# The opening of a top-k attention and gated FFN kernel: loads in the program's order, weight splits behind score evictions, the first unit one step sooner

## The chip, the cores and the metric

One core of one Trainium2 chip. The metric is the device time of one execution in microseconds. The engines are PE (TensorE), DVE (VectorE), ACT (ScalarE), POOL (GpSimd) and SP (SyncE, which here issues nearly all loads).

## What is computed

The reference, cut: attention over 8 batches and 8 heads of 576 positions with 64 columns each. Every row of scores keeps those that are at least its 32nd largest. The result, as a 4608 x 512 matrix, goes through a gated FFN of width 1536.

```python
scores = scale * np.matmul(q, k.transpose(0, 1, 3, 2))
kth = np.partition(scores, -top_k, axis=-1)[..., -top_k:-top_k + 1]
attn = softmax(np.where(scores >= kth, scores, -1e9))
x = np.matmul(attn, v)            # then laid out as (4608, 512)
out = (1 / (1 + np.exp(-(x @ w_gate))) * (x @ w_val)) @ w_out
```

## The kernel before

**Steps.** `run` (L532) goes through 160 steps; a step is a pair of heads `p` (4 of them), and a tile `i` of 128 query rows (tile 4 has 64 rows of each head and counts as one). Names end in `_i_p` (`e_1_3` is tile 1 of the pair 3). In the first batch steps 0 to 7 are tiles 0 and 1 of the four pairs, 8 to 15 tiles 2 and 3, 16 to 19 tile 4. The 256 rows of steps 0 to 7 are the first unit of the FFN.

**One step** passes through four stages on all engines:

- *scores* (L256): PE multiplies (`pss`), ACT evicts to `s` (L270 in the first batch, in two halves).
- *select* (L334): DVE takes the 8 largest of eight segments (`cand`, L351, 16 instructions), and from them the 24 largest of the row (`tops`, `leads`, L355, L357). ACT marks what lies under the 24th (`under`, L364), POOL multiplies (`u`, L370, L371). Then DVE takes the threshold (`kths`, L378). ACT makes the exponentials (`e`, L300), DVE masks and sums them (`masked`, L305 to L309), POOL spreads the inverse sum (`inv`, L311).
- *turn* (L381): PE transposes `e` and `inv` (`pt`, L389, L392), ACT evicts (`et`, L395).
- *weigh* (L415): PE multiplies with the values (`po`, L425), DVE scales (`xf`, L429), ACT and POOL cut that into a high and a low part (`xh` L432, `xl` L433), which are the FFN's input.

At step `n` the loop (L642) puts out the scores of step `n + 2`, the select of `n`, the mask of `n - 1`, the turn of `n - 2` and the weighing of `n - 3`.

**FFN.** `ffn` (L436) is a generator, which `more` (L578) carries on to a goal: a number of rows that follows the attention's progress by the table `PACE` (L78). Its projections are `pz` (L466 to L468: 3 matmuls per slab of 128 inputs, 12 per weight), their gates come from ACT (L473), DVE (L476), ACT (L477) and POOL (L478).

**Weights.** The weights arrive as 64-bit numbers, which must be cut into two parts of 32 bits on the chip: 18 weights in two halves. A half is a *split*: a load (`wraw`, L149), then `split_front` (L151: ACT L168, L173, L176; DVE L169 to L171; POOL L175), then `split_back` (L179: PE `wrest` L183 to L185, ACT L187, a store to `ws`). The splits of the first `LOADED` = 5 weights stand in steps 0 to 9, one half at each, and these weights are loaded again for the first unit (`w_first`, L195, `first_weights` L198). The other weights are split while the first unit's FFN runs and used straight from the split.

**What sets the order.** PE's order is the program's (`manual_schedule`, L628). On the other engines a scheduler places each instruction by its own estimate of times; `urgent` (L124) gives a priority, and `first_scores` (L121) holds an instruction behind the eviction of some scores of the first steps. Loads on SP are placed in the same way. Each engine and SP's queue then runs its list strictly in order: an instruction that waits holds up what is behind it.

## Time and profile before

| | us |
|---|---|
| median of 3 runs | 1597.29 |
| lowest and highest run | 1595.20 and 1598.22 |
| the profiled execution, its own time | 1597.74 |
| its span in the trace | 1595.9 |
| busy in the span: PE, PE weight loads, DVE, ACT, POOL | 1522.6, 1427.3, 1285.6, 1165.3, 1124.2 |

The page's slices (40 us each) show PE at 3, 7, 7 and 8 tenths in the first four and at 9 or more in nearly all others. PE is thus the engine of most of the span, and 73 of its 1595.9 us are idle. DVE is at 6 in the first slice and at 9 or more in the next three.

### The profile page before, as it was taken

Reading aid. Unit: us, or ns where it says so; the run is one execution under the profiler, and the core shown is the slowest. Engines: PE = TensorE matmul, PEld = TensorE weight load, DVE = VectorE, ACT = ScalarE, POOL = GpSimd, SP = SyncE. Lnnn points to the kernel's source line nnn. Section 1 sums busy time; section 2 is a strip of 40 time slices with the busy share of each in tenths; the row PEclk is TensorE's granted clock in tenths of the full one; section 3 lists DMA queues with packets and bytes.
Section 4 is the critical chain, followed back from the end, with each engine's and each line's share of the span. In section 5 each row is a group of like instructions: output and inputs, shape, how many; then the busy total and the mean of one; then the engine's idle time right before and its main releaser. Section 6 shows DMA issues by size and latency. Waiting matters only on the chain.

```text
span 1595.9 us, 36725 instructions
## 1 busy us (share of the span) xinstructions
PE 1522.6 (95%) x11810; PEld 1427.3 (89%) x11810; DVE 1285.6 (81%) x5940; ACT 1165.3 (73%) x2567; POOL 1124.2 (70%) x1747
## 2 busy tenths in 40 slices
PE   3779899999999999999999999999999999999998
PEld 1457679989999999999999999999999999999998
DVE  6999877898998788899899788899899788898001
ACT  5878887788787677787777677787777777777321
POOL 3667896698886786797776886797776786685312
PEclk9989999999999999999999999999999999999999
DMA  7456778777755565666555665666555665554575
GB/s 215 154 197 229 263 263 285 269 246 255 254 194 187 212 240 198 213 211 222 190 200 189 211 242 197 213 213 219 189 200 191 211 226 198 198 192 168 188 267 187
DMA packets 91739, 342.94 MB, mean 215 GB/s; under 512 B 10256, under 2 KB 37392, under 8 KB 63248
## 3 DMA queue, kind: packets, MB, share of 16 engines
q1 hardware_dynamic: 86352, 321.62, 58.2%
q10 hardware_dynamic: 5184, 18.88, 3.0%
q8 instruction: 95, 1.56, 0.4%
q14 instruction: 108, 0.88, 0.2%
HBM read 312.15 MB, written 28.31 MB: 213 GB/s over the span
## 4 chain that ended last, share of the span: by engine, by line
PE 69%; DVE 10%; ACT 3%; POOL 2%; issue 2%; DMA 1%; SPq 0%; ACTq 0%; POOLq 0%; DVEq 0%
PE pz L466 10%; PE pz L468 10%; PE pz L467 10%; PE pss L284 8%; PE po L425 7%; PE pt L389 6%; PE po L490 5%; PE po L492 5%; PE po L491 5%; DVE cand L351 3%; DVE e L305 2%; DVE kths L378 2%; DVE cand L357 1%; PE pt L400 1%; ACT under L364 1%
## 5 line engine op out<-in xcount | busy, mean ns | idle before, releaser
L370 POOL TENSOR_TENSOR u<-s,under 128x288 f32<-128x288 f32 x576 | 420.1, 753 | 98.9 <-ACT under L364 94.4
L466 PE MATMUL pz<-xh,w 128*128 128x384 f32 (+1 forms) x1152 | 404.4, 351 | 1.3 <-DMA w<-ws 1.3
L351 DVE MAX8 cand<-s 128x8 f32<-128x72 f32 x2304 | 348.0, 217 | 70.0 <-ACT s L292 55.8
L468 PE MATMUL pz<-xh,w 128*128 128x384 f32 (+1 forms) x1152 | 377.2, 327 | 0.0
L467 PE MATMUL pz<-xl,w 128*128 128x384 f32 (+1 forms) x1152 | 376.3, 327 | 0.0
L305 DVE SCALAR_TENSOR_TENSOR e<-s,kths,e 128x576 f32<-128x576 f32 x288 | 285.9, 995 | 22.1 <-ACT e L300 21.7
L364 ACT ACTIVATE under<-s,leads 128x576 fp8e4<-128x576 f32 x288 | 222.5, 774 | 95.2 <-DVE leads L355 83.8
L378 DVE MAX8 kths<-u 128x8 f32<-128x584 f32 x288 | 218.9, 760 | 58.9 <-POOL u L371 56.7
L300 ACT ACTIVATE e<-s,st 128x576 f32<-128x576 f32 x288 | 210.5, 771 | 34.3 <-PE pt L389 18.8
L466 PEld LDWEIGHTS pz<-xh,w 128*128 128x128 f32 x1152 | 217.1, 188 | 5.1 <-issue 2.1
L467 PEld LDWEIGHTS pz<-xl,w 128*128 128x128 f32 x1152 | 217.8, 189 | 0.0
L478 POOL TENSOR_TENSOR gl<-gf,gh 128x384 fp32r<-128x384 f32 (+1 forms) x156 | 153.4, 983 | 90.1 <-ACT gh L477 86.8
L468 PEld LDWEIGHTS pz<-xh,w 128*128 128x128 f32 x1152 | 216.6, 188 | 0.0
L395 ACT ACTIVATE et<-pt 128x384 f32<-128x384 f32 (+1 forms) x384 | 197.3, 524 | 20.1 <-PE pt L389 14.8
L490 PE MATMUL po<-gh,w 128*128 128x384 f32 (+1 forms) x576 | 203.9, 354 | 0.8 <-ACT part L505 0.7
L389 PE MATMUL pt<-ident,e 128*128 128x128 f32 x1152 | 191.6, 276 | 9.1 <-ACT et L395 9.0
L491 PE MATMUL po<-gl,w 128*128 128x384 f32 (+1 forms) x576 | 188.6, 328 | 3.1 <-POOL gl L478 3.1
L492 PE MATMUL po<-gh,w 128*128 128x384 f32 (+1 forms) x576 | 189.0, 328 | 0.0
L425 PEld LDWEIGHTS po<-et,v 128*64 128x64 f32 x1600 | 160.4, 137 | 16.5 <-issue 11.6
L425 PE MATMUL po<-et,v 128*64 128x128 f32 (+1 forms) x1600 | 173.5, 265 | 0.0
L426 PE MATMUL po<-et,v 128*64 128x128 f32 (+1 forms) x1600 | 173.5, 265 | 0.0
L389 PEld LDWEIGHTS pt<-ident,e 128*128 128x128 f32 x1152 | 146.0, 141 | 30.4 <-ACT et L395 12.7
(104 smaller groups left out, 3471.0 us busy)
## 6 DMA issues: line engine op xcount, KB each, us to landing
w<-ws SPq DMA_DIRECT2D x216, 1024.0 KB, 4.9
v<-in_v_dram SPq DMA_DIRECT2D x68, 320.0 KB, 3.5
wraw<-in_w_dram SPq DMA_DIRECT2D x36, 512.0 KB, 4.5
ws<-wsplit ACTq DMA_DIRECT2D x36, 512.0 KB, 3.9
qraw<-in_q_dram SPq DMA_DIRECT2D x140, 128.0 KB, 3.5
kraw<-in_k_dram SPq DMA_DIRECT2D x56, 288.0 KB, 3.8
out_dram<-acc SPq DMA_DIRECT2D x40, 192.0 KB, 4.3
w_first<-ws SPq DMA_DIRECT2D x5, 1024.0 KB, 4.8
```

The costliest lines, as they stand in the source:

```text
L305: nc.vector.scalar_tensor_tensor(e[:, j], s[:, j], kth[j], e[:, j], op0=ALU.is_ge, op1=ALU.mult, accum_out=st[:, 4 + j : 5 + j])
L351: nc.vector.max(cand[:, j, 8 * g : 8 * g + 8], s[:, j, g * SEG : (g + 1) * SEG])
L370: nc.gpsimd.tensor_tensor(u[:, j, c], s[:, j, c], under[:, j, c], op=ALU.mult)
L378: nc.vector.max(kths[:, at[j] : at[j] + 8], u[:, j])
L389: nc.tensor.transpose(pt[:, c], ef[:, k0 : k0 + P], ident)
L425: nc.tensor.matmul(po[D:, c], vt[:, 5 + a], et[:, 4 + a, :n], start=a == 0, stop=a == 4)
L466: nc.tensor.matmul(ps[:, R], wt[:, u, 0, d], xh[:, R], start=d == 0, stop=False)
L467: nc.tensor.matmul(ps[:, R], wt[:, u, 0, d], xl[:, R], start=False, stop=False)
L468: nc.tensor.matmul(ps[:, R], wt[:, u, 1, d], xh[:, R], start=False, stop=d == NP - 1)
L490: nc.tensor.matmul(ps[:, R], wts[e // 2][:, e % 2, 0, f], gh[:, R], start=f == 0, stop=False)
L491: nc.tensor.matmul(ps[:, R], wts[e // 2][:, e % 2, 0, f], gl[:, R], start=False, stop=False)
L492: nc.tensor.matmul(ps[:, R], wts[e // 2][:, e % 2, 1, f], gh[:, R], start=False, stop=f == FG - 1)
```

## The change

- `load` issues every load on SP. While `pinned` is set (from the start to step 19, that is until `n == PINNED`), it asks the scheduler to leave the loads in the program's order.
- `load_keys` of the first batch puts off the second head's separate copy of the keys (`later`), which tile 4 alone needs, to steps 8 to 11.
- At step 0 the keys and queries of step 2 are asked for ahead of the first weight.
- `behind_scores` holds the first two ACT instructions of a split (L168, L173) behind the last eviction of scores that the program has put out, for the first twelve evictions. Before, it was the third or fourth eviction of all, for the first eight.
- `LOADED` is 4: two halves of splits leave the first steps and join those beside the FFN.
- Up to `OPEN` = step 9, a step turns `n - 1` and weighs `n - 2` (`lag` 1), its mask of `n - 1` stands ahead of its select, and both halves of the scores come first. Step 9 turns nothing, weighs step 7 and begins the FFN.
- `PACE` begins 32 rows sooner and has 8 rows more at 512.

```diff
-    PACE = [(EARLY, 16), (2 * EARLY, EARLY - 24), (3 * EARLY, 2 * EARLY - 32), (3 * EARLY + BEHIND, 3 * EARLY)]
-    LOADED = 5
+    PACE = [(EARLY - 32, 16), (2 * EARLY, EARLY - 16), (3 * EARLY, 2 * EARLY - 32), (3 * EARLY + BEHIND, 3 * EARLY)]
+    LOADED = 4
+    OPEN = NP * 2 + 1
+    PINNED = 5 * NP
...
+    def behind_scores():
+        return tc.issue_after(evicted[-1].ins) if len(evicted) < 12 else ExitStack()
...
+    def load(dst, src_):
+        ins = nc.sync.dma_start(dst, src_)
+        if pinned:
+            tc.keep_in_program_order(ins)
...
-        with first_scores(idx == i == 0):
+        with behind_scores():
             nc.scalar.activation(bits, top.bitcast(F32), AF.Copy, scale=2.0**-112)
...
-            nc.sync.dma_start(second[:D], k[b, 2 * p + 1][:D])
+            later.append((second[:D], k[b, 2 * p + 1][:D]))
...
         def choose(n):
             nonlocal col
+            if n - 1 in parts and n < OPEN and not general:
+                done[n - 1] = next(parts.pop(n - 1))
             if n < len(steps):
...
+            early = not general and n < OPEN
             splitting = not general and len(fronts) > 0
+            if n == 0:
+                fetch_keys(2)
+                ask(AHEAD)
...
-            if not general and n == NP * len(groups[0][1]) + 2:
+            if n == OPEN and not general:
                 first_weights(0)
...
+            if later and (general or n >= 2 * NP):
+                load(*later.pop(0))
+            if n == PINNED:
+                pinned.clear()
...
-            goal = 0 if at < EARLY else max(at - BEHIND, np.interp(at, *zip(*PACE))) * per_row
-            first, second = begin(n + AHEAD), turned(n - 2) if 2 <= n < len(steps) + 2 else iter(())
+            goal = 0 if n < OPEN else max(at - BEHIND, np.interp(at, *zip(*PACE))) * per_row
+            lag = 1 if early else 2
+            first = begin(n + AHEAD)
+            second = turned(n - lag) if lag <= n < len(steps) + 2 and (early or general or n != OPEN) else iter(())
...
-                if n == NP * len(groups[0][1]) + 2:
-                    chunks = [first, None, second, second, first, second]
+                if early:
+                    chunks = [first, first, None, second, second, second]
+                if n == OPEN:
+                    chunks = [first, None, None, first]
...
-                    elif 3 <= n:
-                        weighed(n - 3)
+                    elif lag + 1 <= n:
+                        weighed(n - lag - 1 if n != OPEN else n - 2)
```

How the lists of the engines move is shown at three places. Line numbers in the lists of the change are its own: up to L270 of before they are 3 to 11 higher, from L284 on 11 higher (a little more past the places of the diff). The last number of a name only tells buffers apart.

**ACT, from the third eviction of scores on.** Before:

```order
L270 ACTIVATE s_0_0_180<-pss_0_0_1_185 128x2x288
L270 ACTIVATE s_1_0_189<-pss_1_0_0_190 128x2x288
L168 ACTIVATE wbits_0_203<-wraw_0_199 128x512
L173 ACTIVATE wsplit_198<-wraw_0_199 128x512
L173 ACTIVATE wsplit_363<-wraw_0_283 128x512
L270 ACTIVATE s_1_0_189<-pss_1_0_1_194 128x2x288
L364 ACTIVATE under_0_0_237,sums_0_0_234<-s_0_0_180,leads 128x576
L176 ACTIVATE wsplit_198<-wbits_0_203 128x512
L364 ACTIVATE under_0_0_237,sums_0_0_234<-s_0_0_180,leads 128x576
L300 ACTIVATE e_0_0_235<-s_0_0_180,st_0_0_233 128x576 x2
```

With the change:

```order
L281 ACTIVATE s_0_0_179<-pss_0_0_1_184 128x2x288
L281 ACTIVATE s_1_0_188<-pss_1_0_0_189 128x2x288
L281 ACTIVATE s_1_0_188<-pss_1_0_1_193 128x2x288
L179 ACTIVATE wbits_0_208<-wraw_0_204 128x512
L184 ACTIVATE wsplit_203<-wraw_0_204 128x512
L375 ACTIVATE under_0_0_234,sums_0_0_231<-s_0_0_179,leads 128x576 x2
L311 ACTIVATE e_0_0_232<-s_0_0_179,st_0_0_230 128x576 x2
L281 ACTIVATE s_0_1_271<-pss_0_1_0_272 128x2x288
L187 ACTIVATE wsplit_203<-wbits_0_208 128x512
L311 ACTIVATE e_1_0_306<-s_1_0_188,st_1_0_304 128x576 x2
```

The third instruction of a split (L173) of the second weight, `wsplit_363<-wraw_0_283`, stood ahead of the eviction of the second half of `s_1_0`. Now all four halves are evicted ahead of any split, and only the first split's two instructions stand ahead of the first tile's `under`.

**PE, from the end of the first unit's last weighing on.** Before:

```order
L425 MATMUL po_1_3_1314<-et_1_3_1213,v_3_803 64x128
L426 MATMUL po_1_3_1314<-et_1_3_1213,v_3_803 64x128
L389 MATMUL pt_2_0_0_1341<-ident,e_2_0_1036 128x128 x3
L389 MATMUL pt_2_0_1_1346<-ident,e_2_0_1036 128x128 x3
L266 MATMUL pss_2_2_1_1351<-k_2_4_224,q_2_2_1030 128x288 x2
L389 MATMUL pt_2_0_2_1355<-ident,e_2_0_1036 128x128 x3
L392 MATMUL pt_2_0_2_1355<-ident,inv_2_0_1206 128x128
L466 MATMUL pz_0_0_0_1364<-xh_0_659,w_first_1240 128x256
L467 MATMUL pz_0_0_0_1364<-xl_0_660,w_first_1240 128x256
L468 MATMUL pz_0_0_0_1364<-xh_0_659,w_first_1240 128x256
L466 MATMUL pz_0_0_0_1364<-xh_1_884,w_first_1240 128x256
L467 MATMUL pz_0_0_0_1364<-xl_1_885,w_first_1240 128x256
```

With the change:

```order
L436 MATMUL po_1_3_1211<-et_1_3_1127,v_3_844 64x128
L437 MATMUL po_1_3_1211<-et_1_3_1127,v_3_844 64x128
L477 MATMUL pz_0_0_0_1240<-xh_0_555,w_first_1144 128x256
L478 MATMUL pz_0_0_0_1240<-xl_0_556,w_first_1144 128x256
L479 MATMUL pz_0_0_0_1240<-xh_0_555,w_first_1144 128x256
L477 MATMUL pz_0_0_0_1240<-xh_1_780,w_first_1144 128x256
L478 MATMUL pz_0_0_0_1240<-xl_1_781,w_first_1144 128x256
L479 MATMUL pz_0_0_0_1240<-xh_1_780,w_first_1144 128x256
```

Before, the transposes of step 8 and a half of the scores of step 12 stood between the weighing `po_1_3` and the first projection. Now the projection follows at once; those come behind 24 and more projections, as do three halves of scores in all, and two of the ten `wrest` of before.

**DVE, where the masks of steps 8 and 9 and the first unit's last `xf` stand.** Before:

```order
L305 SCALAR_TENSOR_TENSOR e_2_0_1036,st_2_0_1034<-s_2_0_858,kths,e_2_0_1036 128x576
L357 MATCH_REPLACE cand_2_1_1250<-tops_2_1_1251,cand_2_1_1250 128x64
L169 TENSOR_SCALAR wbits_1_1620<-wbits_1_1620 128x512
L357 MATCH_REPLACE cand_2_1_1250<-tops_2_1_1251,cand_2_1_1250 128x64
L351 MAX cand_3_1_1405<-s_3_1_1208 128x8 x10
L308 TENSOR_SCALAR st_2_0_1034<-st_2_0_1034 128x2
L355 MAX tops_2_1_1251<-cand_2_1_1250 128x8
L351 MAX cand_3_1_1405<-s_3_1_1208 128x8
L355 MAX tops_2_1_1251<-cand_2_1_1250 128x8
L351 MAX cand_3_1_1405<-s_3_1_1208 128x8 x5
L170 SCALAR_TENSOR_TENSOR wbits_1_1620<-wraw_1_1544,wbits_1_1620 128x512
L378 MAX kths<-u_3_0_1162 128x8
```

With the change:

```order
L440 TENSOR_TENSOR xf_1_2_1008<-po_1_2_1007,et_1_2_914 128x128
L319 TENSOR_SCALAR st_2_0_1071<-st_2_0_1071 128x2
L368 MATCH_REPLACE cand_3_0_1153<-tops_3_0_1154,cand_3_0_1153 128x64
L366 MAX leads<-cand_3_0_1153 128x8
L320 RECIPROCAL st_2_0_1071<-st_2_0_1071 128x2
L366 MAX leads<-cand_3_0_1153 128x8
L389 MAX kths<-u_3_0_1158 128x8 x2
L316 SCALAR_TENSOR_TENSOR e_3_0_1157,st_3_0_1155<-s_3_0_996,kths,e_3_0_1157 128x576 x2
L362 MAX cand_2_1_1288<-s_2_1_1118 128x8 x8
L319 TENSOR_SCALAR st_3_0_1155<-st_3_0_1155 128x2
L362 MAX cand_2_1_1288<-s_2_1_1118 128x8 x8
L320 RECIPROCAL st_3_0_1155<-st_3_0_1155 128x2
```

Before, candidates of later steps and splits stand between the leads (`leads<-cand_3_0`, two rows ahead of these) and the threshold (`kths<-u_3_0`) of step 9. Now the threshold follows the leads at once, and no split stands among these rows.

Taken as groups of neighbouring rows that write one tile, PE's list has some 1810 groups, and behind the first 325 of them it is the same in both kernels.

## Rows read from the trace of the kernel before

**Rows 1.** Windows of the whole core: window, length, busy us (and count) by engine, PEclk, DMA share, GB/s

```profile
0.00:30.00 30.00, 8.38 (x26) 3.46 (x28) 15.88 (x81) 16.51 (x31) 9.46 (x29) 1.00 0.87 243
30.00:112.00 82.00, 60.16 (x371) 35.45 (x370) 81.11 (x393) 66.15 (x133) 51.19 (x81) 0.88 0.49 171
112.00:260.00 148.00, 134.46 (x930) 107.24 (x928) 122.60 (x421) 123.03 (x263) 120.91 (x172) 0.98 0.73 253
260.00:1500.00 1240.00, 1230.84 (x9939) 1193.71 (x9940) 1055.73 (x5027) 940.37 (x2104) 920.17 (x1444) 1.00 0.61 212
```

**Rows 2.** Waits of PE, 0 to 112 us: waiter, releaser, us, times, longest

```profile
PE pss L266 <- ACT s L270: 26.1, 12, 6.6
```

**Rows 3.** Waits of PE, 112 to 260 us

```profile
PE wrest L183 <- ACT wsplit L187: 6.2, 6, 2.0
PE wrest L185 <- POOL wsplit L175: 2.2, 2, 1.3
PE pz L466 <- ACT xh L432: 2.0, 1, 2.0
```

**Rows 4.** Timeline of ACT and DVE, 18 to 20 us: start, us, instructions [idle before]

```profile
18.34 0.66 ACT L173 ACTIVATE wsplit<-wraw 128x512 fp32r<-128x512 uint32 x1 [5.64 <-DMA wraw<-in_w_dram]
19.57 1.18 DVE L351 MAX8 cand<-s 128x8 f32<-128x72 f32 x8 [4.58 <-ACT s L270]
```

**Rows 5.** DVE's instructions by form, 0 to 122 us: count, busy us, mean ns, idle before

```profile
L351 DVE MAX8 cand<-s 128x8 f32<-128x72 f32 x208 | 32.6, 214 | 12.9 <-ACT s L270 12.9
L305 DVE SCALAR_TENSOR_TENSOR e<-s,kths,e 128x576 f32<-128x576 f32 x22 | 21.7, 988 | 0.0
L170 DVE SCALAR_TENSOR_TENSOR wbits<-wraw,wbits 128x512 uint32<-128x512 uint32 x13 | 9.0, 696 | 0.0
L169 DVE TENSOR_SCALAR wbits<-wbits 128x512 uint32<-128x512 uint32 x13 | 6.6, 509 | 1.0 <-ACT wbits L168 1.0
L171 DVE TENSOR_SCALAR wpower<-wbits 128x512 uint16<-128x512 uint16 x11 | 5.0, 458 | 0.0
```

**Rows 6.** Timeline of DVE and POOL, 39 to 60 us

```profile
40.08 0.20 DVE L355 MAX8 leads<-cand 128x8 f32<-128x64 f32 x1
43.79 1.58 DVE L378 MAX8 kths<-u 128x8 f32<-128x584 f32 x2 [0.61 <-POOL u L371]
42.69 0.48 DVE L355 MAX8 leads<-cand 128x8 f32<-128x64 f32 x2
47.44 0.73 POOL L371 TENSOR_TENSOR u<-over,sums 128x16 f32<-128x16 f32 x1
```

**Rows 7.** Timeline of DVE, ACT and PE where the first projection begins

```profile
110.72 0.47 DVE L429 TENSOR_TENSOR xf<-po,et 128x128 f32<-128x128 f32 x2
114.64 0.41 ACT L432 ACTIVATE xh<-xf 128x256 fp32r<-128x256 f32 x1
115.09 0.58 PE L466 MATMUL pz<-xh,w_first 128*128 128x256 f32 x1 [1.96 <-ACT xh L432]
```

**Rows 8.** Timeline of PE, 65 to 69 us

```profile
65.79 0.55 PE L389 MATMUL pt<-ident,e 128*128 128x128 f32 x3 [2.82 <-ACT et L395]
66.18 1.02 PE L183 MATMUL wrest<-wbits,ident 128*128 128x512 f32 x2
67.60 0.76 PE L266 MATMUL pss<-k,q 64*128 64x288 f32 x4
68.28 0.55 PE L389 MATMUL pt<-ident,e 128*128 128x128 f32 x3
```

**Rows 9.** Timeline of SP's queue, at 119 us

```profile
119.29 5.94 SPq L195 DMA_DIRECT2D w_first<-ws  x2
```

**Rows 10.** All `wrest` matmuls, 112 to 260 us: ns min/median/max, first and last start

```profile
L183 PE MATMUL wrest<-wbits,ident x52: 590/592/697, 133.7 to 246.6; 128*128 128x512 f32 x52
```

**Rows 11.** Timeline of POOL, one pair of products each

```profile
25.92 1.87 POOL L370 TENSOR_TENSOR u<-s,under 128x288 f32<-128x288 f32 x2 [2.29 <-ACT under L364]
40.49 1.35 POOL L370 TENSOR_TENSOR u<-s,under 128x288 f32<-128x288 f32 x2
```

More of the change, by code (lines that the diff above doesn't have):

```diff
@@ L135, in tile_topk_attention_then_gated_ffn @@
         order += [] if g == NG - 1 else [(g + 1) * FG + f for f in range(1, FG)]
-    stored, splits, waiting, fetched, ticks, evicted, due = set(), {}, [], {}, [0], [], []
+    stored, splits, waiting, fetched, ticks, evicted, due, later, pinned = set(), {}, [], {}, [0], [], [], [], []
     pre = ExitStack()
@@ L145, in tile_topk_attention_then_gated_ffn @@
     raws = {}
+    def load(dst, src_):
+        ins = nc.sync.dma_start(dst, src_)
+        if pinned:
+            tc.keep_in_program_order(ins)
     def load_raw(idx, i):
         raws[idx, i] = raw = pre_pools["raw"].tile([P, NP * P, 2], U32, tag="raw", name=f"wraw_{idx}_{i}")
-        nc.sync.dma_start(raw.rearrange("p n t -> p (n t)"), w[idx][:, i * NP * P : (i + 1) * NP * P].bitcast(U32))
+        load(raw.rearrange("p n t -> p (n t)"), w[idx][:, i * NP * P : (i + 1) * NP * P].bitcast(U32))
     def split_front(idx, i):
@@ L171, in split_front @@
         nc.vector.tensor_scalar(power.bitcast(U16), heads, 0xFF80, None, op0=ALU.bitwise_and)
-        with first_scores(idx == i == 0):
+        with behind_scores():
             nc.scalar.activation(frac, low, AF.Copy)
@@ L194, in stored_weight @@
         wt = pools["w"].tile([P, 2, 2, NP, P], F32R, tag="w", name=f"w_{nm0}_{idx}")
-        nc.sync.dma_start(wt.rearrange("p i a c n -> p i a (c n)").bitcast(F32), w_split[idx])
+        load(wt.rearrange("p i a c n -> p i a (c n)").bitcast(F32), w_split[idx])
         return wt
@@ L222, in load_keys @@
             both, second = [bk.tile([P, S], F32, tag="k", name=f"k_{nm}_{h}") for h in (2 * p, 2 * p + 1)]
-            nc.sync.dma_start(both[:D], k[b, 2 * p][:D])
-            nc.sync.dma_start(both[D:], k[b, 2 * p + 1][D:])
-            nc.sync.dma_start(second[:D], k[b, 2 * p + 1][:D])
+            load(both[:D], k[b, 2 * p][:D])
+            load(both[D:], k[b, 2 * p + 1][D:])
+            later.append((second[:D], k[b, 2 * p + 1][:D]))
             return [both, second]
@@ L230, in load_keys @@
             raw = bkr.tile([P, S], F32, tag="kraw", name=f"kraw_{nm}_{h}")
-            nc.sync.dma_start(raw, k[b, h])
+            load(raw, k[b, h])
             kt = bk.tile([P, S], F32R, tag="k", name=f"k_{nm}_{h}")
@@ L240, in load_values @@
         vt = bv.tile([P, 10, D], F32, tag="v", name=f"v_{nm}")
-        nc.sync.dma_start(vt, v[b, p].rearrange("p (c d) -> p c d", d=D))
+        load(vt, v[b, p].rearrange("p (c d) -> p c d", d=D))
         return vt
@@ L246, in load_queries @@
             whole = bq.tile([P, 2 * P], F32, tag="qh", name=f"q_{b}_{i}_{p}")
-            nc.sync.dma_start(whole, q[b, i, p])
+            load(whole, q[b, i, p])
             return (whole,)
         raw = bqr.tile([P, 2 * P], F32, tag="qraw", name=f"qraw_{b}_{i}_{p}")
-        nc.sync.dma_start(raw, q[b, i, p])
+        load(raw, q[b, i, p])
         qh, ql = [bq.tile([P, 2 * P], F32R, tag=t, name=f"{t}_{b}_{i}_{p}") for t in ("qh", "ql")]
@@ L630, in run @@
             stated.append(region)
+        if not general:
+            pinned.append(True)
         fetch_keys(0)
@@ L642, in run @@
         for n in range(len(steps) + 3):
+            early = not general and n < OPEN
             splitting = not general and len(fronts) > 0
+            if n == 0:
+                fetch_keys(2)
+                ask(AHEAD)
             if splitting:
                 split_front(*fronts.pop(0))
-            if not general and n == NP * len(groups[0][1]) + 2:
+            if n == OPEN and not general:
                 first_weights(0)
             if n == 0:
-                for m in range(1, KEYS):
+                for m in (1, *range(3, KEYS)):
                     fetch_keys(m)
-                for m in range(AHEAD, ASK):
+                for m in range(AHEAD + 1, ASK):
                     ask(m)
+            if later and (general or n >= 2 * NP):
+                load(*later.pop(0))
+            if n == PINNED:
+                pinned.clear()
             fetch_values(n)
@@ L681, in run @@
                         next(chunk, None)
-                    elif 3 <= n:
-                        weighed(n - 3)
+                    elif lag + 1 <= n:
+                        weighed(n - lag - 1 if n != OPEN else n - 2)
                     if t == 2 and splitting and len(waiting) > 1:
                         split_back()
-                    if chunks[1] is not None or t > 4:
+                    if n != OPEN or t > 0:
                         more(begun + (goal - begun) * (t + 1) / len(chunks))
```

## The prediction

> **What bounds the kernel now.** I read the windows first. From 260 to 1500 us PE is busy 1230.8 of 1240 us [rows 1]: there it sets the pace, and its list there is the same in both kernels. Whatever the change brings must come from the first 260 us. In these PE is busy 8.4 of 30, 60.2 of 82 and 134.5 of 148 us, so 57 of the 73 idle us lie there. From 30 to 112 us it is DVE that sets the pace: 81.1 of 82 us busy [rows 1]. PE's own view says the same from the other side: up to 112 us it waits 26.1 us for evictions of scores [rows 2], which stand in ACT's list behind work that waits for DVE. From 112 us on PE has the projections. Its waits are then no longer on attention but on the splits of weights: 6.2 and 2.2 us ahead of `wrest`, and 2.0 us for the first unit's last slab [rows 3].
>
> So the time of the whole is the time T at which the first unit's last slab reaches PE (115.1 us [rows 7]), plus PE's work behind T, plus its waits behind T. The change moves all three. The sum below is made against the profiled execution's 1597.74 us (span 1595.9), which is 0.45 us above the median of 1597.29.
>
> **The change part by part** (minus is faster).
>
> 1. *Splits behind evictions, loads in order.* ACT stood idle 5.64 us on the load of the second weight, with the eviction of `s_1_0` behind it; DVE waited 4.58 us for that eviction [rows 4]. Now all four first evictions stand ahead of any split. I take the 4.58 us of DVE whole: -4.6. At the least it is -3.6, since the next eviction (`s_0_1`) now stands behind the first tile's signs and exponentials and about 1 us of that can show.
>
> 2. *Less DVE work ahead of the first unit's last `xf`.* DVE runs its list in order. By the two lists, ahead of `xf_1_3` there are 8 candidates, 4 L169, 3 L170 and 2 L171 fewer and one mask more (four short ones cancel). With the means [rows 5] that is 8 x 0.214 + 4 x 0.509 + 3 x 0.696 + 2 x 0.458 - 0.988 = 5.8 us. Neighbouring instructions overlap: eight candidates take 1.18 us [rows 4], not 8 x 0.214 = 1.71. I take three quarters: -4.4 (ends -4.0 and -5.8).
>
> 3. *A lag of one step.* The threshold of a step needs its leads, then ACT, then POOL. From the second leads to the threshold this took 3.5 us in one step, and 5.0 to 5.5 in another (42.69 to the end of POOL's L371 at 48.17) [rows 6]. With two steps of slack DVE had other work meanwhile; it waited 0.6 us [rows 6]. In the new list the work between them is short in six of the first ten steps: eight or sixteen candidates and a few short ones, 2.2 to 3.3 us, and nothing at all in step 9. Against 3.5 us they fall short by 0.8, 0.2, 0.7, 1.3, 1.0 and 3.5, together 7.5 us; against 5.0 by 16.5. The least is the 0.6 us of before. The new wait is not seen in this trace. I take 4.0, the middle of 0.6 and 7.5, as the 3.5 us row is the less loaded case but the scheduler also reorders around the shortfall: +4.0. Behind the waiting threshold stand the next candidates, and for its mask wait PE's transposes.
>
> 4. *xf to xh.* The last `xf` began at 110.72, its `xh` only at 114.64, since ACT's list had scores, a sign and exponentials between; PE took the slab at 115.09 [rows 7]. In the new list ACT has its signs and exponentials ahead of the moment at which `xf` comes. About 1 us of wait is left of 3.4: -2.0 (ends 0 and -3).
>
> So T comes 4.6 + 4.4 - 4.0 + 2.0 = 7.0 us sooner, at about 108.
>
> 5. *PE's work behind T.* What stood ahead of the projections and now stands behind them costs PE time that was idle and is now full: two `wrest` groups of 1.42 us (66.18 to 67.60), three halves of scores of 0.68, ten transposes, 0.39 for three [rows 8]: 2.84 + 2.04 + 1.3 = +6.2. This has one answer, as PE has no slack behind T but its waits.
>
> 6. *Waits behind T.* Of PE's waits on splits (8.4 us in the two rows [rows 3]) I take 3.2 off: the masks of steps 8 and 9 now stand sooner in DVE's list, so that ACT and POOL are less behind with attention when the splits come. At the worst they grow with two halves more among them (28 for 26): +0.7. At the best all of them go.
>
> The rest costs nothing: the keys for tile 4, put off to steps 8 to 11, are needed only for step 16; the other edits of `PACE` move projections between full steps; one reload of a weight less is not waited for.
>
> Sum: -7.0 + 6.2 - 3.2 = -4.0, so 1593.7 for the profiled execution and **1593.3 us** as a median. It is a small rest of large terms, and I say so in the chances. About 0.2%, or 3.2 us, is what a measurement can tell from no change; the forecast is just beyond it.
>
> **POOL beside DVE.** A pair of POOL's products took 1.35 us at 40.49, and 1.87 at 25.92 [rows 11]. The Trainium skill's GPSIMD Engine Reference (Key points) says that GpSimd shares its SBUF interfaces with VectorE, and that DVE instructions with two SBUF inputs contend with it; the mask L305 is one. By that rule the latency in part 3 would be nearer the longer case, since the new list brings masks next to the products that the threshold waits for. The trace has both cases, and the rule speaks against this change.
>
> **Rivals.**
>
> - *The lag costs what the longer latency says* (slower). One mechanism, at DVE's thresholds in steps 2 to 9: with the mean of 3.5 and 5.0 us, the shortfall is 12.0 instead of 4.0, and the sum +4.0: **1601.3**. With 5.0 throughout it is 16.5, thus 1605.8. It decides from 11.2 us on. For it: DVE's list puts the threshold of step 9 directly behind its leads. Against it: before, DVE waited 0.6 us though gaps of 3 us occur there too.
> - *The splits set the pace behind T* (no change). Before, 26 `wrest` groups (two L183 each) spread over 113 us [rows 10], 4.5 us each, and PE waits on them. If that is ACT's, DVE's and POOL's own pace, 28 take 122 us. They begin 7.0 us sooner by T and 2.5 us by PE's list (78 projections ahead of the first of them, 99 before), and 3.3 us later for the moved scores and transposes ahead of it. The last then lies 2.8 us behind where it was: **1600.1**. For it: ACT, DVE and POOL are each busy 121 to 123 of 148 us there [rows 1]. Against it: none is full.
> - *The pinned loads hold each other up* (the change does not do what it says). The fourth `w_first` needs a buffer that the first projections free, and the two such loads of before held SP 5.94 us [rows 9]. Now queries and raw weights stand behind them in fixed order. If ACT waits those 5.6 us again, the gain is gone: **1598.9**.
> - *The waits behind T go altogether*: 8.4 instead of 3.2 us off, 1588.1.
>
> **How the numbers follow.** The forecast (1590 to 1594) has 0.30, the vanishing waits 0.12: faster by over 0.2% is 0.42. Splits that set the pace 0.21 and held-up loads 0.13 make 0.34 for no change. The lag 0.24, slower; the rule on the shared interface and the list of step 9 keep it that high. The range takes in the best case with part 3 at its least up to 1586, and the lag up to 1601.5, which leaves out about 2 in 10. Since no sign has most of the chance by far, the forecast's own range is 1590 to 1596.
>
> **What would show it.** Right: ACT without the 5.64 us wait, DVE's first threshold about 4 us sooner; the first slab of four at 108 us; DVE's idle from 30 to 112 us at 4 to 5 us; PE's waits at `wrest` at 5 us, and 53 us of PE idle by 260. Wrong: waits of `kths` on POOL of over 11 us ahead of the first `xf_1_3`, or a first slab behind 113 us (the lag); `wrest` waits of 9 us or more (the splits); ACT or PE waiting on loads behind 60 us (the pinned order). A difference behind 300 us would overthrow the whole frame.

## The result and the profile after

The change is **slower** by 1.0%: a median of 1613.07 us (1610.1 to 1617.03, 4 runs) beside 1597.45 us for the kernel before. The ratio is 1.0102, with a 95% interval from 1.0073 to 1.0131, so 12 to 21 us. Forecast were 1593.3 us and a range up to 1601.5. Both the sign and the range were wrong.

Lines of the code after stand 11 further on than those of before from L266 on (L266 is now L277; a little more in `run`), and all plain loads stand on L154. First the windows of the whole core, in the columns of [rows 1]:

```profile
0.00:30.00 30.00, 14.53 (x42) 6.44 (x42) 21.27 (x110) 18.57 (x35) 11.91 (x33) 1.00 0.60 179
30.00:112.00 82.00, 54.18 (x270) 33.81 (x271) 66.07 (x311) 53.78 (x109) 41.82 (x71) 0.70 0.35 126
112.00:260.00 148.00, 135.75 (x895) 104.61 (x894) 121.59 (x434) 120.48 (x252) 103.45 (x150) 0.96 0.71 243
260.00:1500.00 1240.00, 1226.11 (x9942) 1187.40 (x9942) 1065.20 (x5063) 946.44 (x2120) 933.77 (x1465) 1.00 0.61 214
```

In the first 30 us every engine gets more done than before. The loss is in the second row: DVE was busy 81.1 of 82 us [rows 1] and is busy 66.1 now, PE does 270 matmuls there and not 371, and its granted clock falls from 0.88 to 0.70, a mixture of the levels 2.4 and 1.2 GHz. Both programs issue 11810 matmuls, so the time of the k-th from the last can be set side by side. Against before, the change is 11.3 us ahead at the 11,700th from the last, which before began at 59.5 us, and 16.0 us behind at the 11,500th, which before began at 95.7. At the 10,100th (300 us) it is 16.8 behind and at the 500th 18.9. All but 3 us of it is lost while the change goes from 48 to 112 us. The opening's lists differ in order, so a single point of this comparison is rough there (20.2 us behind at the 11,200th, 11.0 at the 10,800th).

Second, PE's waits from 30 to 112 us (waiter, releaser, us in total, times, longest). Before, then with the change:

```profile
PE pss L266 <- ACT s L270: 13.0, 7, 4.0
PE pt L389 <- ACT et L395: 9.0, 6, 3.6
```

```profile
PE pss L277 <- ACT s L281: 16.1, 7, 4.3
PE pt L400 <- ACT et L406: 12.8, 5, 4.7
```

DVE's waits from 0 to 125 us, before and with the change:

```profile
DVE cand L351 <- ACT s L270: 12.9, 3, 7.5
DVE kths L378 <- POOL u L371: 1.1, 2, 0.6
```

```profile
DVE cand L362 <- ACT s L281: 18.1, 12, 7.0
DVE kths L389 <- POOL u L382: 9.5, 6, 3.7
```

PE waits for evictions of scores and of transposes in turn, as it did before, and a little longer (3.1 and 3.8 us). What is new is DVE. Between 30 and 112 us it waited 0.6 us for thresholds before and never for scores; now it waits 6.3 us for thresholds and 8.4 us for scores. PE's waits, which had cost nothing while DVE had work, now reach DVE. One step of the change, from the timelines of PE and of ACT (start, us, instruction, idle before in brackets):

```profile
63.91 2.32 PE L400 MATMUL pt<-ident,e 128*128 128x128 f32 x9
66.03 0.31 PE L403 MATMUL pt<-ident,inv 128*128 128x128 f32 x1
66.27 0.76 PE L277 MATMUL pss<-k,q 64*128 64x288 f32 x4
71.37 1.33 PE L277 MATMUL pss<-k,q 64*128 64x288 f32 x4 [4.34 <-ACT s L281]
```

```profile
66.66 0.48 ACT L406 ACTIVATE et<-pt 128x384 f32<-128x384 f32 x1
68.34 1.44 ACT L311 ACTIVATE e<-s,st 128x576 f32<-128x576 f32 x2 [1.20 <-POOL st L370]
69.69 0.57 ACT L406 ACTIVATE et<-pt 128x512 f32<-128x512 f32 x1
70.16 0.61 ACT L187 ACTIVATE wsplit<-wbits 128x512 fp32r<-128x512 f32 x1
70.68 0.64 ACT L281 ACTIVATE s<-pss 128x576 f32<-128x576 f32 x1
```

PE has done all ten transposes and the first half of the scores by 67.0. There is one score buffer (`pss`), and in the new order of a step the second half is the next entry of PE's list, so PE stands until the first half is evicted. In ACT's list that eviction comes behind the evictions of the transposes that PE has just done, a pair of exponentials that waits for POOL, and a split. In the order of before, two thirds of the transposes stood between the two halves on PE.

Last, the end of the first unit's attention, to set beside [rows 7] (DVE, ACT and PE):

```profile
117.22 0.49 DVE L440 TENSOR_TENSOR xf<-po,et 128x128 f32<-128x128 f32 x2 [0.22 <-PE po L437]
118.29 0.40 ACT L443 ACTIVATE xh<-xf 128x256 fp32r<-128x256 f32 x1
118.74 0.38 PE L477 MATMUL pz<-xh,w_first 128*128 128x256 f32 x1 [0.31 <-ACT xh L443]
121.34 0.58 PE L478 MATMUL pz<-xl,w_first 128*128 128x256 f32 x1 [2.23 <-POOL xl L444]
```

T, the time at which the last slab reaches PE, is 118.74 us. It was 115.09, and 108 was forecast.

### The profile page after: what moved, and what is told of

It reads as the page before. It is cut to its first block, busy times and chain, and to the rows that moved or that the text cites. A ratio compares the mean times of both kernels' runs of the same rounds, so it can differ in the third digit from the quotient of the medians.

```text
span 1615.2 us, 36689 instructions
## 1 busy us (share of the span) xinstructions
PE 1538.5 (95%) x11810; PEld 1438.4 (89%) x11810; DVE 1285.5 (80%) x5940; ACT 1166.6 (72%) x2567; POOL 1120.2 (69%) x1747
## 4 chain that ended last, share of the span: by engine, by line
PE 68%; DVE 9%; ACT 3%; POOL 3%; issue 2%; DMA 1%; POOLq 0%; ACTq 0%; DVEq 0%
PE pz L477 10%; PE pz L479 10%; PE pz L478 10%; PE pss L295 8%; PE po L436 7%; PE pt L400 5%; PE po L501 5%; PE po L503 5%; PE po L502 5%; DVE cand L362 2%; DVE e L316 2%; DVE kths L389 2%; POOL u L381 1%; DMA w<-ws 1%; ACT under L375 1%
## 5 line engine op out<-in xcount | busy, mean ns | idle before, releaser
L316 DVE SCALAR_TENSOR_TENSOR e<-s,kths,e 128x576 f32<-128x576 f32 x288 | 280.7, 979 | 26.4 <-ACT e L311 25.8
L436 PEld LDWEIGHTS po<-et,v 128*64 128x64 f32 x1600 | 164.4, 140 | 17.4 <-issue 12.8
L437 PE MATMUL po<-et,v 128*64 128x128 f32 (+1 forms) x1600 | 177.7, 269 | 0.0
L436 PE MATMUL po<-et,v 128*64 128x128 f32 (+1 forms) x1600 | 177.7, 269 | 0.0
```

The source lines that it names most:

```text
L316: nc.vector.scalar_tensor_tensor(e[:, j], s[:, j], kth[j], e[:, j], op0=ALU.is_ge, op1=ALU.mult, accum_out=st[:, 4 + j : 5 + j])
L436: nc.tensor.matmul(po[D:, c], vt[:, 5 + a], et[:, 4 + a, :n], start=a == 0, stop=a == 4)
```

## The experiments

Two theories came out of the traces, and a third from the prediction. **L**: the turned, shorter lag costs (later split into L1, the lag itself, and L2, the order of the step: which parts of a step stand between the two halves of its scores in PE's list). **P**: the transfers that are held in the program's order hold each other up. **S**: splits of weights set the pace. All of e1 to e18 ran beside the kernel before, which had a median of 1596.06 us there (15 runs); the change itself has only its own four runs, which spread over 7 us, so a difference of a run to the change is good to some 5 us. "Start" means held transfers (loads kept in the program's order), later second keys, earlier keys and queries of step 2, and splits ("half passes" in the expectations) behind evictions, together. "Lag" means the turning one or two steps behind, with what goes along with it in the change: the mask ahead of the select, the FFN's begin at step 9 in place of 10, and the `PACE` of the change.

| run | lag | order of the step | held up to step | weights split first | median us | ratio to before (95%) |
|---|---|---|---|---|---|---|
| before | 2 | old | old start | 5 | 1596.06 | 1 |
| change | 1 | new | 20 | 4 | 1613.07 | 1.0102 (1.0073 to 1.0131) |
| e1 | 2 | old | 20 | 4 | 1606.5 | 1.0074 (1.0062 to 1.0087) |
| e2 | 1 | new | old start | 5 | 1620.78 | 1.0157 (1.0142 to 1.0172) |
| e3 | 1 | new | none | 4 | 1612.61 | 1.0118 (1.0101 to 1.0135) |
| e4 | 1 | new | 20 | 5 | 1620.68 | 1.0161 (1.0147 to 1.0174) |
| e5 | 2 | old | 8 | 4 | 1592.37 | 0.9975 (0.9965 to 0.9985) |
| e6 | 2 | old | 20 | 5 | 1601.15 | 1.0029 (1.0020 to 1.0038) |
| e7 | 1 | old | 20 | 4 | 1601.12 | 1.0036 (1.0024 to 1.0048) |
| e8 | 2 | new | 20 | 4 | 1623.16 | 1.0167 (1.0152 to 1.0182) |
| e9 | 1 | old | 8 | 4 | 1592.12 | 0.9979 (0.9969 to 0.9989) |
| e10 | 1 | new | 8 | 4 | 1613.23 | 1.0117 (1.0102 to 1.0132) |
| e11 | 1 | one third between | 20 | 4 | 1598.76 | 1.0019 (1.0010 to 1.0028) |
| e12 | 2 | old | 8 | 5 | 1589.6 | 0.9968 (0.9958 to 0.9978) |
| e13 | 1 | new, 8 extra | 20 | 4 | 1602.26 | 1.0040 (1.0026 to 1.0054) |
| e14 | 1 | one third between | 8 | 5 | 1595.13 | 0.9995 (0.9986 to 1.0004) |
| e15 | 1 | old | old start | 5 | 1596.28 | 1.0000 (0.9991 to 1.0009) |
| e16 | 1 | new, 2 extra | 20 | 4 | 1611.8 | 1.0098 (1.0083 to 1.0113) |
| e17 | 2 | old, 4 extra | 8 | 5 | 1587.6 | 0.9949 (0.9935 to 0.9963) |
| e18 | 2 | old, 8 extra | 8 | 5 | 1593.09 | 0.9981 (0.9972 to 0.9990) |

### Which part costs: e1 to e4

e1, the start alone: the turning, its order, the FFN's earlier begin and `PACE` undone (against the change, cut).

```diff
-    PACE = [(EARLY - 32, 16), (2 * EARLY, EARLY - 16), (3 * EARLY, 2 * EARLY - 32), (3 * EARLY + BEHIND, 3 * EARLY)]
+    PACE = [(EARLY, 16), (2 * EARLY, EARLY - 24), (3 * EARLY, 2 * EARLY - 32), (3 * EARLY + BEHIND, 3 * EARLY)]
...
-    OPEN = NP * 2 + 1
+    OPEN = NP * 2 + 2
...
-            lag = 1 if early else 2
...
+            first, second = begin(n + AHEAD), turned(n - 2) if 2 <= n < len(steps) + 2 else iter(())
...
-                if early:
-                    chunks = [first, first, None, second, second, second]
...
+                    chunks = [first, None, second, second, first, second]
```

> The change without its turned and shorter lag: transfers in the program's order, half passes behind evictions, four weights split at the start, turning and weighting two steps behind as before. If the shorter lag costs the 16 us (theory L), this run keeps the 5 us that the first two steps gained and loses nothing: 1590 to 1596 us, TensorE's granted clock between 30 and 112 us near 0.88, VectorE idle less than 20 us by 120 us. If the order of the transfers holds loads up (theory P), the first gate weights are still behind one another: 1605 to 1615 us. If the weights that are split later set the pace (theory S): 1602 to 1608 us.

e2, the turning alone: the kernel before with the lag and order of the change, and with what goes along with the lag (the two lines that count, as an edit of the kernel before).

```diff
+            lag = 1 if early else 2
...
+                if early:
+                    chunks = [first, first, None, second, second, second]
```

> The kernel before with the shorter lag and its order of the step alone: transfers, half passes and five weights as before. Theory L: 1612 to 1620 us, with VectorE waiting 10 us or more for scores in the first 125 us and a granted clock of 0.70 between 30 and 112 us. Theories P and S: 1594 to 1599 us, as before or a little less.

e3, no transfer held:

```diff
-        if not general:
-            pinned.append(True)
```

> The change with the opening's transfers free to stand where the scheduler puts them. Theory P: the three gate weights at 95.5 us no longer hold the queue for 17.5 us and the time falls to 1598 to 1604 us. Theories L and S: 1610 to 1618 us, and the first step may be later again.

e4, five weights:

```diff
-    LOADED = 4
+    LOADED = 5
```

> The change with five weights split at the start, as before, in place of four. Theory S: 1600 to 1606 us, since two half passes fewer stand between 112 and 260 us. Theory L: within 4 us of the change (1609 to 1617 us), with the last slab of the first unit 2 to 4 us later. Theory P: the gate weights still stand behind one another in the queue, so likewise 1609 to 1617 us.

e2 carries more than the whole loss, as L said: 25 us. But e1 loses 12 us (by the ratio) with the old turning, where L had a gain, so there are **two causes**. In e1 PE was 8.1 us ahead at the 10,700th matmul from the last (236 us before) and 9.4 us behind at the 10,300th (280 us), a loss of 17.5 us. This is where the largest piece went, PE's timeline first, then the queue of SP, which issues the loads (start, time that the issue took, transfers), and last the longest wait of that queue between 200 and 260 us:

```profile
245.76 1.22 PE L194 MATMUL wrest<-wbits,ident 128*128 128x512 f32 x1 [7.54 <-DVE wbits L181]
```

```profile
234.98 0.33 SPq L154 DMA_DIRECT2D v<-in_v_dram  x1
235.40 1.03 SPq L154 DMA_DIRECT2D kraw<-in_k_dram  x2
236.48 0.42 SPq L154 DMA_DIRECT2D qraw<-in_q_dram  x1
237.07 0.33 SPq L154 DMA_DIRECT2D wraw<-in_w_dram  x1
```

```profile
SPq L154 <- PE po L437: 19.6, 2, 16.5
```

The queue issued nothing from 218.4 to 235.0 us. At its head stood a load of values (`v`), whose buffer PE's weighing (`po`) had not yet freed, and keys, queries and a raw weight (`wraw`) stood behind it. So `wraw` is asked for only at 237.07, and the split that PE's list needs next waits for it. PE's waits for queries of the second batch near 265 us (3.6 and 1.6 us) are a smaller piece of the loss. In the kernel before two keys of the second batch were asked for at 17.0 us already. e3 says that the change itself suffers little from the held order, as it is like the change; e4 that a fifth weight makes it worse by 7.6 us, against S.

### Held transfers and the order of a step: e5 to e8

e5, the start alone with transfers held up to step 8 (`PINNED = 2 * NP` in place of `5 * NP`):

```diff
-    PINNED = 5 * NP
+    PINNED = 2 * NP
```

> The start alone (turning two steps behind, as before), with its transfers held in the program's order up to step 8 in place of step 20. The start alone was 7 to 8 us ahead of the kernel before up to 236 us, then TensorE stood 7.5 us at a split whose raw weight had been asked for only at 237 us, behind eight second-batch keys and queries, and 9.4 us of lead became as much behind. If the held order makes that (theory P), the lead stays: 1586 to 1591 us, faster than both kernels. If the four weights and the splits behind them make it (theory S), the wait stays near 245 us: 1602 to 1608 us.

e6, e1 with `LOADED = 5`:

```diff
-    LOADED = 4
+    LOADED = 5
```

> The start alone with five weights split at the start in place of four, all transfers held up to step 20. Theory S (the splits left for later set the pace): two half passes fewer stand between 112 and 260 us, 1592 to 1598 us. Theory P (the held order): the second batch's keys still stand ahead of the raw weights, 1602 to 1610 us.

e7, the change with the old order of a step, lag of one kept:

```diff
-                    chunks = [first, first, None, second, second, second]
+                    chunks = [first, second, second, first, None, second]
```

> The change with the shorter lag, but with the order of a step as before: one half of the scores, two thirds of the turning, the other half of the scores, the weighting, the last third. If the lag itself costs (theory L1: the threshold waits for its leads and the transposes for the mask in the same step), 1608 to 1618 us. If the order costs (theory L2: both halves of the scores ahead of the transposes, so that the second waits for the eviction of the first, which stands behind evictions of transposes in ScalarE's list), most of the loss goes: 1596 to 1604 us, with less than 10 us of TensorE's wait for the eviction of scores between 30 and 112 us (16.1 in the change).

e8, e1 with the new order of a step, lag of two kept:

```diff
+                if n < OPEN:
+                    chunks = [first, first, None, second, second, second]
```

> The start alone, turning two steps behind, but with the change's order of a step (both halves of the scores first, then the weighting, then the turning). Theory L1: as the start alone, 1604 to 1610 us. Theory L2: 1612 to 1622 us, with the loss between 48 and 112 us.

e7 gives back 12 us and e8 loses 17 more than e1: the **order costs, whichever lag it goes with**. With the lag of two, e8's thresholds too wait for POOL (5.3 us from 30 to 112 us), as the change's do. (e7's wait for evictions of scores fell to 11.2 us, not below 10 as L2 had it.) e5 gains 14 us on e1 by the shorter hold and is faster than the kernel before; its queue asks for the raw weights in good time, one by one between keys. Its load of values comes no sooner (236.45 us), but no raw weight stands behind it any more:

```profile
215.42 0.33 SPq L154 DMA_DIRECT2D kraw<-in_k_dram  x1
215.86 0.36 SPq L154 DMA_DIRECT2D wraw<-in_w_dram  x1
216.32 0.38 SPq L154 DMA_DIRECT2D qraw<-in_q_dram  x1
218.06 0.33 SPq L154 DMA_DIRECT2D kraw<-in_k_dram  x1
```

e6 fell between P and S. It still loses 16 us between 236 and 280 us, so the hold is the larger part there.

### Do they add up: e9 to e12

e9 joins the edits of e5 and e7 to the change; e10 has that of e5 alone; e11 puts one third of the turning back between the halves; e12 is e5 with five weights. In this order:

```diff
-    PINNED = 5 * NP
+    PINNED = 2 * NP
-                    chunks = [first, first, None, second, second, second]
+                    chunks = [first, second, second, first, None, second]
```

> The change with the order of a step as before and with transfers held only up to step 8: both mended edits at once, so that against the start with step 8 (1592.4 us) only the lag of one step is left. If the lag by itself is free once scores and transposes alternate, 1588 to 1593 us. If it costs as the run with the old order of a step suggests (there TensorE was 15 us ahead at its 110th matmul and 3 us behind at its 510th), 1596 to 1602 us.

```diff
-    PINNED = 5 * NP
+    PINNED = 2 * NP
```

> The change, with transfers held only up to step 8 in place of step 20. The start alone gained 14 us by this. In the trace of the change TensorE does not have the 7.5 us wait for a raw weight near 245 us, since its weights there stand ahead of the second batch's keys; so if that wait was the whole of theory P, the change gains little: 1609 to 1614 us. If held transfers also slow the change between 95 and 130 us (gate weights that hold the queue for 17.5 us), 1600 to 1607 us.

```diff
-                    chunks = [first, first, None, second, second, second]
+                    chunks = [first, second, first, None, second, second]
```

> The change with one third of the turning put back between the two halves of the scores (half, third, half, weighting, third, third); lag and transfers as in the change. If the loss comes from there being nothing for TensorE to do while the first half's eviction frees the one score buffer (theory L2), one third between regains most of the 12 us that the whole old order regained: 1600 to 1606 us. If it is the place of the weighting or of the other thirds, 1609 to 1615 us.

```diff
-    LOADED = 4
+    LOADED = 5
```

> The start with transfers held up to step 8, with five weights split at the start in place of four. With transfers held up to step 20 five were 5.4 us better than four. If that was theory S, five are again better: 1586 to 1590 us. If it was only that fewer raw weights stood behind the second batch's keys, which step 8 has mended already, 1591 to 1597 us.

e11 is the sharpest of these: **one third of the transposes between the two halves** takes back 14 us (1613.1 to 1598.8), with lag, hold and the place of the weighing as good as unchanged. Its waits from 30 to 112 us:

```profile
PE pss L277 <- ACT s L281: 12.3, 6, 4.0
DVE kths L389 <- POOL u L382: 1.7, 3, 0.6
DVE cand L362 <- ACT s L281: 1.3, 2, 0.7
```

The scheduler also put ACT's list in another order in e11. But it did not evict the first halves sooner: between 30 and 112 us these evictions began on average 2.0 us behind the end of PE's half in e11 and 1.6 us in the change (worked out from the two timelines). PE had other work in the meantime, and DVE's wait for scores fell from 8.4 to 1.3 us.

e9 equals e5, with the lag and what goes along with it as the difference between them, so these are free there. With the same order in both, no pair shows the lag to cost: e7 is 5 us faster than e1 and the change 10 us faster than e8. e10 equals the change within its 5 us: while the order costs, the hold costs nothing on top, as its first reading had it; the two losses do not simply add. In e12 the fifth weight tends to help (0.9968 against 0.9975, with intervals that overlap).

### The lag by itself, the clock, and the best version: e13 to e18

e15 is the kernel before with a lag of one (and what goes along with it) and the old order. Of its edit the line that differs from e2's:

```diff
+                if early:
+                    chunks = [first, second, second, first, None, second]
```

> The kernel before with the lag of one step alone and the order of a step as before: transfers, half passes and five weights as in the kernel before. The same with the change's order of a step took 1620.8 us. If the lag by itself is free and the order is all (theory L2), 1594 to 1600 us. If the lag costs wherever the start does not make up for it, 1603 to 1612 us.

It took 1.0000 times the time of before. DVE's waits in it, 0 to 125 us:

```profile
DVE cand L362 <- ACT s L281: 11.9, 3, 7.4
DVE wbits L180 <- ACT wbits L179: 1.8, 2, 1.0
DVE kths L389 <- POOL u L382: 1.3, 2, 0.7
```

The thresholds (`kths`) wait 1.3 us for POOL, where the change's waited 9.5. The wait that I had priced comes with the order, not with the lag.

e13 puts work of no use where PE waits:

```diff
+                        if early and t == 0 and n > 0:
+                            fill = ps_f.tile([P, NP * P], F32, tag="f", name=f"fill_{n}")
+                            for _ in range(8):
+                                nc.tensor.matmul(fill[:, :P], ident, ident, start=True, stop=True)
```

> The change with eight extra transposes of the identity, read by nobody, on TensorE between the two halves of the scores in each step 1 to 8. They are work of no use and stand where TensorE waits for the eviction (0.7 to 4.3 us a step); by the rows of the change eight such instructions take 1.1 us at 2.4 GHz and 1.8 us at 1.2 GHz. If the granted clock follows what TensorE does and the 16 us of longer matmuls are a cause of their own (theory C), the clock between 30 and 112 us rises from 0.70 to 0.80 or more and the time falls to 1603 to 1609 us. If the half clock only accompanies the waits (theory F), the extra work is hidden where the wait is long and costs 1 to 2 us in the three steps where it is short: 1612 to 1618 us.

e16 has two of them a step in place of eight (`range(2)`):

```diff
-                            for _ in range(8):
+                            for _ in range(2):
```

> The change with two extra transposes of the identity a step in place of eight. With eight, the other engines' lists were put in another order too, so that the 11 us gained there may be the clock's or the order's; with two, VectorE's and SyncE's lists are those of the change and ScalarE's nearly so. By the eight (2.05 us a step at 2.4 GHz) two take 0.5 us. Theory C (the clock by itself): a granted clock between 30 and 112 us above 0.75 goes with a time below 1609 us, and where it stays near 0.70 the time stays at 1611 to 1615 us. If the order made the gain of the eight, the time stays at 1611 to 1616 us whatever the clock does.

Windows from 30 to 112 us of e13 and of e16, in the columns of [rows 1]:

```profile
30.00:112.00 82.00, 64.37 (x470) 47.09 (x470) 70.95 (x350) 60.33 (x122) 47.17 (x79) 0.94 0.41 144
```

```profile
30.00:112.00 82.00, 58.68 (x348) 38.60 (x350) 68.62 (x330) 56.02 (x113) 42.38 (x73) 0.77 0.39 141
```

e13's clock rose to 0.94, and 10 of the 16 us came back. But the scheduler had also put the lists of ACT and DVE in another order; in ACT's, for one, an eviction of scores moved ahead of a split. In e16 the lists of ACT and DVE are those of the change up to some 97 us and differ in a few places behind, the clock rose to 0.77, and the time did not move beyond the intervals. Theory C had asked for less than 1609 us above 0.75, so it failed there. That the **clock by itself** gives back time is not shown; at 0.94 it can't be told from the order of ACT's list.

e14 joins e11 with the shorter hold and five weights:

```diff
-    PINNED = 5 * NP
+    PINNED = 2 * NP
-    LOADED = 4
+    LOADED = 5
```

> The shorter lag with a third of the turning between the halves, transfers held up to step 8, five weights. By the sums of the runs so far (a third between was 2.4 us better than the whole old order, step 8 gained 9.0 us with the old order, five weights gained 2.8 us at lag two) it comes to 1587 to 1591 us, beside 1589.6 us for the best so far. If five weights cost under the shorter lag, as they did in the change (7.6 us), 1594 to 1599 us.

It missed its sum by 4 us and fell to the second reading, that five weights cost under a lag of one; that was not separated further. Last, e12 with four and with eight extra transposes behind the first half of the scores:

```diff
+                        if not general and n < OPEN and t == 0 and n > 0:
+                            fill = ps_f.tile([P, NP * P], F32, tag="f", name=f"fill_{n}_{t}")
+                            for _ in range(4):
+                                nc.tensor.matmul(fill[:, :P], ident, ident, start=True, stop=True)
```

> The best version so far (the start with transfers held up to step 8, five weights, 1589.6 us; granted clock 0.83 between 30 and 112 us), with four extra transposes of the identity behind the first half of the scores in steps 1 to 9, 1.0 us each at 2.4 GHz. Here the transposes of the step before stand behind them, so they are not all in a gap. Theory C: the clock there rises to 0.9 or more, and 1584 to 1588 us. If VectorE, 81.2 of 82 us busy there, sets the pace whatever TensorE's clock is, 1588 to 1592 us.

> As the run with four, with eight a step (2.05 us each). Theory C, with TensorE short of work in that stretch: 1583 to 1588 us. With VectorE as the pace and the extra work in the way of the transposes: 1589 to 1596 us.

e17 is **the best version**, 8 us (6 to 10) faster than the kernel before. Its window from 30 to 112 us:

```profile
30.00:112.00 82.00, 65.78 (x447) 44.48 (x445) 81.97 (x400) 69.36 (x142) 51.93 (x82) 0.90 0.60 201
```

e17 lies in theory C's range, with the clock at 0.90, and e18 outside it. In e17 DVE is busy 82.0 of 82 us, so the opening is back at the pace that DVE sets. Eight (e18) cost 5.5 us against four, as the second reading had it; its granted clock was 0.92, so the higher clock did not help there. The other engines' lists differ here too, so the 2 us between e12 and e17 are not put down to the clock.

## Why the prediction was wrong

**The frame held.** The difference arose ahead of 260 us and grew by only 2 to 3 us behind 300 us, and PE sets the pace from 260 us on.

**Part 1** (splits behind evictions, -4.6) was right. The first threshold comes at 18.93 us in place of 23.83 and ACT's wait of 5.64 us [rows 4] is gone. e12, which has the start with a short hold and five weights as before, gained 5.1 us (3.5 to 6.7) as a whole.

**Part 2** (less DVE work, -4.4) can't be read in the change, as DVE was no longer what T waited for.

**Part 3 failed, and with it the sum.** It took the turning for a matter of the lag: DVE's thresholds against POOL's products, +4.0. The lag costs nothing (e15, e9 against e5), and the thresholds' wait, 9.5 us in the change, is 1.3 us in e15 with the lag alone. What costs is the order in which a step is written, both halves of the scores ahead of the transposes, and that I had not priced at all. It is 12 us (e7 against the change), 17 (e8 against e1), 21 (e10 against e9) or 24.5 (e2 against e15), by the company that it keeps. The row was there: PE's 26.1 us of waits for evictions of scores [rows 2]. I read it as a sign that DVE set the pace, which was right for the kernel before, and did not ask what PE did between the two halves and whether DVE would go on covering the waits. The PE rows show it: in [rows 8] transposes and a split stand ahead of a half and transposes behind it. The price is not PE's own wait: that rose by 3.1 us from 30 to 112 us. It is what comes of it for DVE, which lost 15 us of work there. The Trainium skill's Perfetto Trace Analysis (Optimizing Tensor Performance, Matmuls) asks that independent matmul groups rotate through PSUM banks, so that the eviction of one overlaps the next. Here the scores have one buffer and transposes stood in for a second; e11 agrees with the rule, with 14 us for one third put back.

**Part 4** (`xf` to `xh`, -2.0) was right, with 2.9: 0.6 us are left between the end of `xf` at 117.71 and `xh` at 118.29. Most of it was lost again just behind T, since the slab's low part then waits 2.23 us for POOL, where it waited 0.22 before.

**T** was therefore 118.7 and not 108.1. These 10.7 us are nearly half of the miss of 23.3 us in the profiled execution (1617.0, where the sum gave 1593.7). The rest lies behind T, and both parts there were too low. **Part 5** (+6.2): PE's busy time behind T rose by 10.4 us (1453.0 to 1463.4). The matmuls that it names did move, 30 in all; the granted clock was lower there too (0.96 from 112 to 260 us, 0.98 before), which the sum left out. **Part 6** (-3.2): PE's idle time behind T did not fall but rose by 5.2 us (27.9 to 33.1). The waits at `wrest` fell as forecast in sign (3.8, 2.2 and 0.8 us in the three largest rows, where 6.2 and 2.2 stood [rows 3]), but others came: 2.2 us for the slab's low part, 3.0 us for queries and 2.1 us for evictions of transposes. What brought these was not separated. The three terms, 10.7 + 4.2 + 8.4, are the whole miss.

One thing hides this from whoever counts waits alone, as I had. PE's busy time in the whole run rose from 1522.6 to 1538.5 us with the same matmuls, and its idle time only from 73.3 to 76.7. By 260 us PE had been idle 55.5 us, less than the 57 of before and near the 53 that were to show me right. At a granted clock of 0.70 a loss shows as longer matmuls: the mean transpose up to 130 us took 348 ns and not 317.

**The rivals.** "The lag costs" had the right sign by the wrong mechanism, and its price (1601.3 to 1605.8) was too low. Of its two signs one came true, a first slab behind 113 us, and the other nearly (9.5 us of `kths` waits, where over 11 were asked for), so the signs could not tell the lag from the order that came with it. "The splits set the pace" forecast no change, and e4, with two splits fewer behind T, was slower and not faster. "The pinned loads hold each other up" is true of the program, with a price of 9 us (e7 against e9) and 14 us (e1 against e5), but in the change it lies under the other loss (e3, e10), and its main place was not the gate weights at 119 us that I named but the second batch's values and what stood behind them up to 235 us. e5 to e9 make it the second cause that the change would meet as soon as the first is mended.

**What stays open:** the clock's own share; what brought the new waits behind T; where e9 gains the rest on e7 (it is ahead by 3 us at 132 us and 8 us at 166 us on the scale of before); and why five weights cost 7.6 us in the change and nothing under a lag of two.

## What to carry to other kernels

Where a result buffer has one copy, look at what stands in the producing engine's list between two uses of it: here that work hid the eviction. Moving it is not priced by the producer's own wait, which rose by 3 us where the order cost 12 to 24.5; look at who is fed by it, and whether that engine stays busy. A queue that is held in the program's order should be held no longer than the stretch that needs it, since a load that waits for its buffer there holds up all that were written behind it (16.5 us in e1). And when TensorE's clock is below full, add its busy time to the account beside its waits, or the loss does not show up where one looks.

## What the hardware showed that was not expected

The eight extra multiplications by the identity showed as 16 instructions, one every 0.13 us, 2.05 us in all at the higher clock, where three transposes of tiles of that size show as three [rows 8]; I had taken 1.1 us for eight. One group of e13 fell on a lower granted clock (0.71 between 64 and 68 us) and took 3.27 us.

```profile
63.73 3.27 PE L712 MATMUL fill<-ident 128*128 128x128 f32 x16
75.32 2.05 PE L712 MATMUL fill<-ident 128*128 128x128 f32 x16
```

With 20.5 us of such work up to 130 us the granted clock between 30 and 112 us was 0.94 and not 0.70, with 7.1 us (two a step) 0.77, and with 12.4 us in the best version 0.90 and not 0.83. Work in the gaps thus went with a higher granted clock over the whole stretch each time, though what that gives back was not shown, and in e13 and e17 the other engines' lists had moved as well.
